# Seven small products for gate/up product 5 too, shared buffers for the small forms, and fewer sums of right operands on VectorE

## The chip, the core and the metric

The kernel runs on one core of one Trainium2 chip. A core has five engines with queues of their own: TensorE (PE; its weight loads are PEld), VectorE (DVE), ScalarE (ACT), GpSimd (POOL) and SyncE (SP). TensorE reads SBUF and writes PSUM, which here is used as eight banks of 128 x 512 float32. SyncE issues the plain loads of this kernel, GpSimd its stores and the transfers that add to what is at the destination ("accumulating"). The metric is the time of one execution in microseconds on the device, as the median of a few runs.

## The reference

```python
a = jnp.einsum("bsd,ed->bse", x, dft_hid_re)
b = jnp.einsum("bsd,ed->bse", x, dft_hid_im)
y = jnp.einsum("ts,bse->bte", dft_seq_re, a) - jnp.einsum("ts,bse->bte", dft_seq_im, b)

gate = jnp.einsum("bsd,df->bsf", x, W_gate)
up = jnp.einsum("bsd,df->bsf", x, W_up)
h = gate * (gate > 0) * up
down = jnp.einsum("bsf,fd->bsd", h, W_down)

g = sigmoid((x * gate_w).sum(-1, keepdims=True))
out = g * y + (1 - g) * down
```

x is 1 x 2048 x 512, W_gate and W_up are 512 x 1792, W_down is 1792 x 512, the sequence matrices are 2048 x 2048 and the hidden ones 512 x 512; all is float32.

## The kernel before

**Three passes for one product.** TensorE multiplies in float32r. Each operand is split into a rounded part ("h", a ScalarE cast) and the rest ("l", a VectorE subtraction of that cast), and a product of two operands is made of three matmuls (`PARTS`): l by h, h by l, h by h.

**Seven products for eight.** Every large product is made as a 2 x 2 of blocks by Winograd's form: products 1 to 7 of sums of blocks in the order `ORDER` = 1, 5, 6, 2, 7, 3, 4. Partial results are carried from one product to the next in PSUM: ScalarE "seeds" a new bank with an old one's contents (`seed`, rows c<-c), and the next product adds to it.

**Stages.** The work goes in this order: (1) `Block`: gate and up for a pair c of 128-wide blocks of the 1792 columns (c = 0 to 6) and a row half q (0 or 1), each with h = relu(gate) * up, stored to `hd` by `h_out`; (2) `SpectralBlock`: x by the hidden matrices, stored to `ad`; one more `Block`; (3) `Down`, twice: h by W_down; (4) `Joint` J1, `Sequence` S00 and S01, J3, S11, S10, J2: the sequence matrices by the results of (2). The trace names them by their tiles: c for (1), a for (2), z for `Down` and `Sequence`, jA to jH for `Joint`.

**The second level.** For c = 3 to 6 product 1 of both row halves together is itself made by seven small products: `RightOne` builds the sums of x, `One` the sums of the weights (wn, split to wnt) and runs seven products of 3 matmuls each; `WEAVE` says after which products of the block before they run. Its results `o[q]` (tile p) are copied by ScalarE into the banks of the blocks (`seed_of`, rows c<-p), which then skip product 1.

**Right operands of the last stages.** A block of `Joint` or `Sequence` needs sums of blocks of the sequence matrices. `SUMS` lists those made beforehand on the chip: 4 loads, 4 VectorE sums (p<-p,p) and 4 stores to `tb`. `DSUMS` lists those made in DRAM by GpSimd alone (`copied_sums`): 4 copies and 4 accumulating transfers from DRAM to DRAM. The key behind each is its place on the planner's scale (one unit is one matmul). A block of a `Sequence` that is in neither list is summed in place (`rights`): three loads r11, r12 and r22, three VectorE sums (r<-r,r) and one accumulating load into r11. What is in a list is loaded from tb, four loads and no sum. Next come the split casts ch and cl; ll and lh are the split of the left operands lr, loaded from ad.

**What sets the order.** All instructions are recorded as steps with a key, in matmuls. The class `Plan` gives each a due time, schedules them on the engines and on 51 buffers ("units") by its own costs, and issues them in the order of the starts it found. `AT` holds key offsets.

Of the kernel before, what the change touches and what calls it, by code (L numbers as in the profile page):

```python
# [347 lines left out]
def kernel(ctx: ExitStack, tc, xP, xG, wgu, wd, cr, ci, wri, gw, out):  # L348
# [55 lines left out]
    class Pair:  # L404


        def __init__(self, name):
            self.name, self.banks = name, None
# [19 lines left out]
    def load(o, i):  # L428
        plan.sync.dma_start(o, i)
# [88 lines left out]

    AT = {'open': (-19, 11, 33, 19, 97), 'w0': (17, 83, 110), 'x': (-192, -134, -93, -86, -59, -42, 27, 18), 'gate': (66, 44, 474), 'v': (-90, -80, -68, -38, -22, 4, 10, 42, 44), 'lw': (-246, -150, -138, -114, -112, -104), 'll': (-90, 62, 36, 96, 138, 176), 'l0': (-154, -42, -52, 32), 'l1': (-60, -118, -28, 40), 'z': (38,), 'J1': (88, 14, 76, 56, 124), 'J2': (174, 18, 40, 44, 52), 'J3': (168, 22, 62, 62, 52), 'hr': (52, 48, 61), 'rest': (26, 46), 'gated': (1880, 1930, 1968, 2012), 'xt': (-20, 26, 62), 'p': (62, 44, 32, 16), 'hs': (8, 6)}

    SUMS = {(0, 3, 1): 1764, (0, 1, 0): 865, (0, 2, 1): 665, (0, 3, 0): 965, (1, 1, 0): 1600, (1, 2, 1): 1632, (1, 5, 3): 1310, (1, 4, 2): 1070, (0, 4, 0): 489, (0, 1, 1): 125, (1, 4, 3): 1730}

    DSUMS = {(0, 2, 0): 290, (1, 2, 0): 100, (1, 3, 1): 417, (1, 3, 0): 675, (1, 1, 1): 520}

# [4 lines left out]
    def h_out(q, c, h, key):  # L529
# [16 lines left out]
        for n, t, k in ((1, h[1], 3), (3, f[0], 8), (5, f[1], 14))[:3 - q]:  # L546
            op(key + k, lambda n=n, t=t: store(hd[q, n:n + 2, :, c].rearrange("x p n -> p x n"), t.all))

    class RightOne:

        def __init__(self, key):
            self.x = buf("x011")
            self.raw = [buf(f"xt{n}") for n in range(2)]
            self.t = [[buf(f"xt{n}{y}", dtype=F32R) for y in "hl"] for n in range(2)]
            x, y, r = self.x, piece[1, "11"], self.raw
            op(key, lambda: load(x.all, xP[0, 0]))
            for n, (o, a, b) in enumerate(((r[0][:, 0], y[:, 0], y[:, 1]), (r[0][:, 1], x[:, 0], y[:, 0]),
                                           (r[1][:, 0], r[0][:, 1], y[:, 1]), (r[1][:, 1], r[1][:, 0], x[:, 1]))):
                op(key + AT["xt"][1] + 2 * n, lambda o=o, a=a, b=b: E().vector.tensor_add(o, a, b))
            for n in range(2):  # L560
                hi, lo = self.t[n]
                op(key + AT["xt"][2] + 10 * n, lambda n=n, hi=hi: E().scalar.copy(hi.all, r[n].all))
                op(key + AT["xt"][2] + 10 * n + 5, lambda n=n, hi=hi, lo=lo: E().vector.tensor_sub(lo.all, r[n].all, f32(hi.all)))

        def of(self, m):
            if m in (1, 2, 3):
                q, k = {1: (0, 0), 2: (0, 1), 3: (1, 1)}[m]
                return [X[q, 1][y][:, k] for y in range(2)]
            n, k = {7: (0, 0), 5: (0, 1), 6: (1, 0), 4: (1, 1)}[m]
            return [self.t[n][y][:, k] for y in range(2)]  # L570

    class One:

        SLOT = {5: 0, 7: 1, 6: 2, 3: 3}

        def __init__(self, w, right, key):
            self.w, self.right = w, right
            self.raw, self.t = buf("wn", [4, P]), buf("wnt", [2, 4, P], F32R)
            self.o = [buf("p") for q in range(2)]
            self.s = buf("ps")  # L580
            self.b = {}
            f, a = self.raw, lambda i, k: w.raw[0][:, i, k]
            for n, (o, x, y) in enumerate(((f[:, 0], a(1, 0), a(1, 1)), (f[:, 1], a(1, 0), a(0, 0)),
                                           (f[:, 2], a(0, 0), f[:, 0]), (f[:, 3], a(0, 1), f[:, 2]))):
                op(key - AT["p"][1] + 2 * n, lambda o=o, x=x, y=y: E().vector.tensor_sub(o, x, y))
            op(key - AT["p"][2], lambda: E().scalar.copy(self.t[:, 0], f.all))
            op(key - AT["p"][3], lambda: E().vector.tensor_sub(self.t[:, 1], f.all, f32(self.t[:, 0])))

        def left(self, m):
            if m in (1, 2, 4):  # L590
                i, k = {1: (0, 0), 2: (0, 1), 4: (1, 1)}[m]
                return [w[:, k] for w in self.w.of(1, i)]
            return [self.t[:, y, self.SLOT[m]] for y in range(2)]
# [20 lines left out]
        def evac(self, m):  # L614
            e, o, s, y, bank = E(), self.o, self.s[:, 0], self.s[:, 1], self.bank

            def seed(k, i, scale):
                self.new(k)
                e.scalar.activation(bank(k), bank(i), AF.Copy, scale=scale)

            if m == 1:
                seed("X", "A", -1.0)
            elif m == 5:
                e.scalar.copy(y, bank("B"))
            elif m == 6:
                seed("D", "X", 1.0)
                e.scalar.copy(s, bank("X"))
            elif m == 2:
                e.scalar.copy(o[0][:, 0], bank("A"))
            elif m == 7:  # L630
                seed("G", "D", -1.0)
                e.vector.tensor_add(o[1][:, 1], bank("D"), y)
            elif m == 3:
                e.vector.tensor_add(o[1][:, 0], bank("B"), s)
            elif m == 4:
                e.scalar.copy(o[0][:, 1], bank("G"))

    class Block:
# [8 lines left out]

        def run(self, order=ORDER, one=None, part=None):
            if part:
                self.part = part.o[self.q]  # L650
                for k in "AX":
                    op(plan.now, self.seed_of, k)
            for m in order:
                for i in range(2):
                    pe(6, self.product, m, i)
                    op(plan.now, self.evac, m, i)
                    if one and (m, i) in WEAVE:
                        one.run(*WEAVE[m, i])
            h_out(self.q, self.w.c, self.h, plan.now + (8 if plan.now > 270 else 100))
# [15 lines left out]

        def seed_of(self, k):
            self.ps[k].new()
            for i in range(2):
                E().scalar.copy(self.ps[k][i], self.part[:, i])

        def resume(self, key):
            op(key, self.seed_of, "X")
            self.run(ORDER[1:3] + ORDER[4:])
# [11 lines left out]
        def evac(self, m, i):  # L695
# [24 lines left out]
            elif m in (3, 7):  # L720
                o, ps, t = (h[0][:, 1], p["B"], self.s) if m == 3 else (h[1][:, 1], p["D"], self.y)
                e.vector.tensor_add(t[:, 0] if i == 0 else o, ps[i], t[:, i])
                if i:
                    e.vector.scalar_tensor_tensor(o, t[:, 0], 0.0, o, op0=OP.max, op1=OP.mult)


    WEAVE = {(7, 1): (1,), (3, 0): (6, 2), (4, 0): (5, 7), (4, 1): (3, 4)}

# [312 lines left out]
    class Sequence(Round):  # L1041
# [29 lines left out]
        def rights(self):  # L1071
# [5 lines left out]
            for jj in range(4):  # L1077
# [9 lines left out]
                for b, t in (("12", 110), ("22", 105), ("11", 90 if m else 100)):  # L1087
                    x = (6 if b == "11" else 7) if m else 5
                    op(at[x, jj] - t, lambda r=r, b=b, jj=jj: load(r[b].all, source(b, jj)))

# [278 lines left out]
    for b, f in (("11", pairs[0]), ("21", pairs[1])):  # L1369
        for k, w in zip(halves, (w0, w1)):  # L1370
# [4 lines left out]
            else:  # L1375
                op(-99, w.load, 0, f)
    for f, *a in ((x_load, 0, "12"), (w2.load, 0), (w0.load, 1), (x_load, 0, "22"), (w1.load, 1), (w2.load, 1), (lambda: load(gwt[:], gw),)):
        op(-98, f, *a)
# [35 lines left out]
    def blocks(sequence):  # L1414
        ones = {}
        for n, (c, q) in enumerate(sequence):
# [3 lines left out]
            if d > 2 and d != c:  # L1420
                if d == 3:
                    right = RightOne(plan.now + AT["xt"][0])
                base = plan.now + (60 if c < 3 else 48)
                w_prep(ws.setdefault(d, Weights(d)), base + 45, early=AT["p"][0])
                one = ones[d] = One(ws[d], right, base)
            if (c, q) == (2, 1):
# [119 lines left out]
```

## Time and profile before

| | |
|---|---|
| median of 3 runs | 775.47 us (775.25 to 776.31) |
| the profiled execution | 775.92 us; its span 774.1 us |
| granted TensorE clock | 1.000 |
| instructions on PE, DVE, ACT, POOL | 3392, 812, 713, 204 |
| HBM | read 189.01 MB, written 94.38 MB |
| TensorE busy by its pieces of the chain | c to 330, then c again to 349, z (`Down`) 349 to 482, J1 to 520, S00 and S01 to 607, J3 to 645, S11 and S10 to 732, J2 to 771 us |

All rows of the profile carry line 125, since every step is issued by one line of `Step.run`; groups are told apart by their tiles, written out<-in. The rows of the prediction come from the page, the waits (who waited, for whom, how long in all, how often), the chain that ended last, windows of the span, groups by form (count, busy time and mean ns of one, then the engine's idle time before them and what ended it), and timelines (start, length, engine, instruction).

### The profile page before, as it was taken

Reading aid. Unit: us, or ns where it says so; the run is one execution under the profiler, and the core shown is the slowest. Engines: PE = TensorE matmul, PEld = TensorE weight load, DVE = VectorE, ACT = ScalarE, POOL = GpSimd, SP = SyncE. Lnnn points to the kernel's source line nnn. Section 1 sums busy time; section 2 is a strip of 40 time slices with the busy share of each in tenths; the row PEclk is TensorE's granted clock in tenths of the full one; section 3 lists DMA queues with packets and bytes.
Section 4 is the critical chain, followed back from the end, with each engine's and each line's share of the span. In section 5 each row is a group of like instructions: output and inputs, shape, how many; then the busy total and the mean of one; then the engine's idle time right before and its main releaser. Section 6 shows DMA issues by size and latency. Waiting matters only on the chain.

```text
span 774.1 us, 10131 instructions
## 1 busy us (share of the span) xinstructions
PE 768.3 (99%) x3392; PEld 634.1 (82%) x3392; DVE 698.6 (90%) x812; ACT 500.0 (65%) x713; POOL 141.3 (18%) x204
## 2 busy tenths in 40 slices
PE   8999999999999999999999999999999999999998
PEld 6878888887888888888888888888888888888887
DVE  6999878676778976999889999999999999999997
ACT  6765474747475644686464668957567886566873
POOL 0133533343223223310202010001010001111000
PEclk9999999999999999999999999999999999999999
DMA  8765999999799999999999999999959899999994
GB/s 322 262 179 177 327 351 343 318 383 292 297 318 419 290 394 420 418 391 406 386 408 419 412 410 392 401 410 412 294 173 338 312 409 358 305 344 296 344 367 96
DMA packets 83683, 263.08 MB, mean 340 GB/s; under 512 B 8624, under 2 KB 19632, under 8 KB 83632
## 3 DMA queue, kind: packets, MB, share of 16 engines
q1 hardware_dynamic: 48048, 162.17, 54.3%
q0 software_dynamic: 35440, 100.15, 42.2%
q8 instruction: 26, 0.43, 0.2%
q14 instruction: 25, 0.20, 0.1%
q10 hardware_dynamic: 144, 0.13, 0.0%
HBM read 189.01 MB, written 94.38 MB: 366 GB/s over the span
## 4 chain that ended last, share of the span: by engine, by line
PE 90%; DVE 5%; DMA 2%; ACT 1%; issue 1%; SPq 1%; ACTq 0%; DVEq 0%
PE z L125 40%; PE c L125 26%; PE a L125 10%; PE jB L125 4%; PE jA L125 4%; DMA wr<-wgu 2%; PE jX L125 2%; PE jD L125 2%; PE jG L125 1%; DVE wr L125 1%; PE jH L125 1%; DVE h L125 1%; DVE p L125 1%; DVE xl L125 1%; SPq L125 1%
## 5 line engine op out<-in xcount | busy, mean ns | idle before, releaser
L125 PE MATMUL z<-cl,lh 128*128 128x512 f32 x452 | 175.9, 389 | 0.0
L125 PE MATMUL z<-ch,ll 128*128 128x512 f32 x452 | 175.8, 389 | 0.0
L125 PE MATMUL z<-ch,lh 128*128 128x512 f32 x452 | 175.8, 389 | 0.0
L125 DVE TENSOR_TENSOR jcl<-jr,jch 128x1024 fp32r<-128x1024 f32 x84 | 98.7, 1221 | 1.2 <-ACT jch L125 1.1
L125 PEld LDWEIGHTS z<-cl,lh 128*128 128x128 f32 x452 | 84.8, 188 | 17.8 <-DVE cl L125 0.2
L125 PEld LDWEIGHTS z<-ch,lh 128*128 128x128 f32 x452 | 84.8, 188 | 17.6
L125 PEld LDWEIGHTS z<-ch,ll 128*128 128x128 f32 x452 | 84.8, 188 | 17.6
L125 ACT CAST ch<-r 128x1024 fp32r<-128x1024 f32 x64 | 66.2, 1053 | 43.5 <-DVE r L125 30.0
L125 ACT CAST jch<-jr 128x1024 fp32r<-128x1024 f32 x84 | 84.8, 1056 | 8.7 <-PE z L125 4.0
L125 DVE TENSOR_TENSOR cl<-r,ch 128x1024 fp32r<-128x1024 f32 x64 | 77.3, 1220 | 0.8 <-ACT ch L125 0.6
L125 ACT CAST ch<-hr 128x1024 fp32r<-128x1024 f32 (+1 forms) x56 | 51.5, 942 | 29.0 <-PE z L125 17.7
L125 ACT ACTIVATE c<-c 128x512 f32<-128x512 f32 x74 | 43.0, 585 | 41.8 <-PE c L125 30.3
L125 DVE TENSOR_TENSOR cl<-hr,ch 128x1024 fp32r<-128x1024 f32 (+1 forms) x56 | 59.6, 1086 | 5.0 <-ACT ch L125 3.1
L125 DVE TENSOR_TENSOR p<-p,p 128x1024 f32<-128x1024 f32 x44 | 53.5, 1220 | 5.0 <-DMA p<-ci 2.7
L125 POOL DMA_DIRECT2D tb<-p x48 | 26.7, 555 | 142.8 <-DVE p L125 131.0
L125 PE MATMUL c<-xh,w2l 128*128 128x512 f32 x112 | 43.7, 390 | 0.2 <-ACT g L125 0.2
L125 PE MATMUL c<-xh,w1l 128*128 128x512 f32 x112 | 43.8, 391 | 0.0
L125 PE MATMUL c<-xl,w1h 128*128 128x512 f32 x112 | 43.6, 389 | 0.0
L125 PE MATMUL c<-xl,w2h 128*128 128x512 f32 x112 | 43.6, 389 | 0.0
L125 PE MATMUL c<-xh,w2h 128*128 128x512 f32 x112 | 43.6, 389 | 0.0
L125 PE MATMUL c<-xh,w1h 128*128 128x512 f32 x112 | 43.6, 389 | 0.0
L125 PE MATMUL a<-vh,xl 128*128 128x512 f32 x112 | 43.6, 389 | 0.0
(196 smaller groups left out, 1686.7 us busy)
## 6 DMA issues: line engine op xcount, KB each, us to landing
tb<-p POOLq DMA_DIRECT2D x48, 512.0 KB, 8.5
jr<-tb SPq DMA_DIRECT2D x48, 512.0 KB, 9.3
hr<-hd SPq DMA_DIRECT2D x36, 512.0 KB, 8.7
ad<-a POOLq DMA_DIRECT2D x28, 512.0 KB, 8.5
p<-cr SPq DMA_DIRECT2D x24, 512.0 KB, 8.5
tb<-ci POOLq DMA_DIRECT2D x24, 512.0 KB, 11.7
hd<-hs POOLq DMA_DIRECT2D x21, 512.0 KB, 10.6
r<-cr SPq DMA_DIRECT2D x21, 512.0 KB, 12.6
```

Of the source, the lines that this page charges most:

```text
L125: getattr(getattr(nc, self.engine), self.name)(*map(ap, self.a), **{k: ap(x) for k, x in self.k.items()})
```

## The change

Product 5 of c = 3 to 6 gets the same treatment as product 1. `RightOne` and `One` take the product's number m. The block of q = 0 weaves the seven small products of its own product 5 (`fives[c]`) between its other products, in the order 2, 6, 7, 3, 4; the block of q = 1 weaves those of the next pair's product 1 between 2, 6, 3, 7, 4. The results of product 5 come back as a second `part`, copied into bank B, so that a block of c = 3 to 6 has five products of its own.

Buffers: the sums of weights are kept in `gwt` (the gate weights are now loaded after the last block), the results share the tiles p, one of the small right operands is written over the halves of X[1, 1] and X[1, 5], which `forms_again` restores from the input (two loads, one difference, two casts, two subtractions).

Right operands: `SUMS` falls from 11 entries to 6 and `DSUMS` rises from 5 to 8; (0, 4, 0) of S00 and (1, 4, 2) of S10 are in neither list any more. `ONTO` names three blocks, (0, 0, 1) and (0, 0, 2) of S00 and (1, 0, 1) of S10, in which one of the three VectorE sums is an accumulating load into r12 instead. Many offsets of `AT` are others.

```diff
-    SUMS = {(0, 3, 1): 1764, (0, 1, 0): 865, (0, 2, 1): 665, ...
+    ONTO = {(0, 0, 1): 50, (0, 0, 2): 50, (1, 0, 1): 42}
+    SUMS = {(0, 3, 1): 1754, (0, 3, 0): 100, (1, 1, 0): 1690, (1, 5, 3): 1600, (0, 1, 1): 1582, (1, 4, 3): 1230}
...
+    def forms_again(key):
+        r = buf("x011")
+        for j in range(2):
+            op(key, lambda j=j: load(r[:, j], xP[2 + j, 0, :, 0]))
+        op(key + 30, lambda: E().vector.tensor_sub(r[:, 1], r[:, 1], r[:, 0]))
+        for j, m in enumerate((1, 5)):
+            hi, lo = (z[:, 0] for z in X[1, m][:2])
+            op(key + 30 + 8 * j, lambda j=j, hi=hi: E().scalar.copy(hi, r[:, j]))
+            op(key + 34 + 8 * j, lambda j=j, hi=hi, lo=lo: E().vector.tensor_sub(lo, r[:, j], f32(hi)))
...
     class RightOne:
-        def __init__(self, key):
+        def __init__(self, m, key, step, both=None):
...
+            if both:
+                self.t[1] = both.t[1]
+            x, y, r = self.x, X[1, m][2], self.raw
+            if m == 1:
+                op(key, lambda: load(x.all, xP[0, 0]))
+            else:
+                op(key, lambda: E().vector.tensor_add(x.all, *(f32(z.all) for z in X[0, m][:2])))
...
+            to = [(r[0].all, [z.all for z in self.t[0]]), (r[1][:, 0], [z[:, self.k] for z in self.t[1]]),
+                  (r[1][:, 1], [z[:, 0] for z in X[1, m][:2]])]
...
     class One:
-        def __init__(self, w, right, key):
+        def __init__(self, w, right, key, step):
-            self.raw, self.t = buf("wn", [4, P]), buf("wnt", [2, 4, P], F32R)
+            self.t = buf("wnt", [2, 4, P], F32R)
             self.o = [buf("p") for q in range(2)]
-            self.s = buf("ps")
...
     class Block:
-        def run(self, order=ORDER, one=None, part=None):
-            if part:
-                self.part = part.o[self.q]
+        def run(self, order=ORDER, one=None, weave=None, parts=()):
+            if parts:
+                self.part, self.y = (p.o[self.q] for p in parts)
                 for k in "AX":
-                    op(plan.now, self.seed_of, k)
+                    op(plan.now, self.seed_of, k, self.part)
             for m in order:
+                if m == 3 and parts:
+                    op(plan.now - 12 * self.q, self.seed_of, "B", self.y)
                 for i in range(2):
                     pe(6, self.product, m, i)
...
-    WEAVE = {(7, 1): (1,), (3, 0): (6, 2), (4, 0): (5, 7), (4, 1): (3, 4)}
+    WEAVE = {1: {(7, 1): (1,), (3, 0): (6, 2), (4, 0): (5, 7), (4, 1): (3, 4)},
+             5: {(2, 0): (1,), (2, 1): (6, 2), (6, 0): (5, 7), (6, 1): (3, 4)},
+             0: {(3, 1): (1,), (7, 0): (6, 2), (7, 1): (5, 7), (4, 0): (3, 4)}}
...
                 for key, o, a, b, sign in sums:
+                    if (m, self.p, jj) in ONTO and (o, a, b) == ("12", "12", "22"):
+                        key = max(key - ONTO[m, self.p, jj], at[5, jj] - 39 if not m else 0)
+                        op(key, lambda r=r, jj=jj: accumulate(r["12"].all, source("22", jj)))
+                        continue
                     op(key, lambda r=r, o=o, a=a, b=b, sign=sign: combine(r[o].all, r[a].all, r[b].all, sign))
...
-            if c in ones:
-                Block(q, ws[c]).run(ORDER[1:], one, ones[c])
-            else:
-                Block(q, ws[c]).run(ORDER, one)
+            if c not in ones:
+                Block(q, ws[c]).run(ORDER, one, WEAVE[1])
+                continue
+            if q == 0:
+                if c == 3:
+                    five = RightOne(5, plan.now + AT["xt5"][0] - 30, (10, 40 + AT["xt5"][1]), right)
+                fives[c] = One(ws[c], five, plan.now + 6, AT["p5"])
+            Block(q, ws[c]).run((2, 6, 3, 7, 4) if q else (2, 6, 7, 3, 4), one if q else fives[c], WEAVE[0 if q else 5],
+                                (ones[c], fives[c]))
...
+    forms_again(plan.now + AT["again"][0])
+    op(plan.now - 60, lambda: load(gwt.all, gw))
```

The programs differ by instructions as follows: 12 matmuls fewer; on VectorE 20 sums p<-p,p fewer, 3 sums r<-r,r more, 24 differences of 128 x 128 more and 16 others more; on ScalarE 12 seeds c<-c, 16 copies c<-p and 10 others more. SyncE issues 20 transfers fewer, GpSimd 9 more.

ScalarE at the start of the first block of c = 3, before. p_969 is the result of the small products of product 1, the c on the left are the banks of the new block.

```order
L125 COPY c_1027<-p_969 128x512
L125 COPY p_969<-c_1003 128x512
L125 COPY c_1041<-p_969 128x512
L125 COPY c_1048<-p_969 128x512
L125 CAST w3_1053<-wr3_1033 128x512
L125 COPY y_1059<-c_1030 128x512
L125 COPY y_1059<-c_1046 128x512
```

The same place in the changed program; p_981 is that result, xt0h and wnt are operands of small products, xh5 one of the overwritten halves.

```order
L125 CAST xt0h_1025<-xt0_961 128x1024
L125 CAST wnt_1033<-gwt_73 128x512
L125 COPY p_981<-c_1009 128x512
L125 COPY c_1043<-p_981 128x512
L125 COPY c_1050<-p_981 128x512
L125 ACTIVATE c_1057<-c_1046 128x512
L125 COPY c_1062<-p_981 128x512
L125 CAST xh5_563<-xt1_969 128x512
L125 ACTIVATE c_1075<-c_1057 128x512
```

The copies of product 5 to y are gone from the block; seeds of the small products (c_1057, c_1075) and casts for them stand among the block's own seeds, and the block's first product is now one that adds to a seeded bank.

VectorE at the start of S00, before, from behind the last jcl of J1. Tiles r_ come from tb, r11, r12 and r22 are summed in place.

```order
L125 TENSOR_TENSOR cl5_4685<-r_4574,ch5_4659 128x1024
L125 TENSOR_TENSOR r11_4562<-r11_4562,r12_4537 128x1024
L125 TENSOR_TENSOR r11_4588<-r11_4588,r12_4570 128x1024
L125 TENSOR_TENSOR cl5_4708<-r11_4562,ch5_4699 128x1024
L125 TENSOR_TENSOR jo1_4719<-jD_4516,js_4547 128x512
L125 TENSOR_TENSOR jo1_4719<-jB_4403,js_4547 128x512
L125 TENSOR_TENSOR cl5_4730<-r11_4588,ch5_4710 128x1024
L125 TENSOR_TENSOR r11_4604<-r11_4604,r12_4594 128x1024
L125 TENSOR_TENSOR ll7_4751<-lr7_4614,lh7_4723 128x1024
L125 TENSOR_TENSOR r12_4537<-r12_4537,r22_4550 128x1024
L125 TENSOR_TENSOR cl5_4772<-r11_4604,ch5_4755 128x1024
```

The same place in the changed program.

```order
L125 TENSOR_TENSOR r11_4579<-r11_4579,r12_4553 128x1024
L125 TENSOR_TENSOR r11_4607<-r11_4607,r12_4588 128x1024
L125 TENSOR_TENSOR cl5_4727<-r11_4579,ch5_4721 128x1024
L125 TENSOR_TENSOR cl5_4737<-r11_4607,ch5_4730 128x1024
L125 TENSOR_TENSOR r11_4633<-r11_4633,r12_4615 128x1024
L125 TENSOR_TENSOR jo1_4754<-jD_4558,js_4583 128x512
L125 TENSOR_TENSOR jo1_4754<-jB_4440,js_4583 128x512
L125 TENSOR_TENSOR cl5_4767<-r11_4633,ch5_4757 128x1024
L125 TENSOR_TENSOR r11_4652<-r11_4652,r12_4640 128x1024
L125 TENSOR_TENSOR r12_4553<-r12_4553,r22_4575 128x1024
L125 TENSOR_TENSOR cl5_4793<-r11_4652,ch5_4784 128x1024
```

All four blocks of S00 are now summed in place, so the first cl5 has two sums ahead of it and the loads of the fourth block stand ahead of the left operands (lr7, lr6) on SyncE. Up to the second cl6 of the stage VectorE has two instructions of 128 x 1024 more than before.

GpSimd at the same place, before:

```order
L125 DMA out<-z12_4453 128x1024
L125 DMA zd_70<-jo1_4719 128x1024
L125 DMA zd_70<-jo0_4628 128x1024
L125 DMA r11_4562<-cr 128x1024
L125 DMA r11_4588<-cr 128x1024
L125 DMA r11_4604<-cr 128x1024
```

And in the changed program:

```order
L125 DMA out<-z12_4482 128x1024
L125 DMA r12_4588<-cr 128x1024
L125 DMA zd_70<-jo0_4660 128x1024
L125 DMA zd_70<-jo1_4754 128x1024
L125 DMA r12_4615<-cr 128x1024
L125 DMA r11_4579<-cr 128x1024
L125 DMA r11_4607<-cr 128x1024
```

Two accumulating loads into r12 stand around the two stores of J1's results, ahead of those into r11.

More of the change, by code (lines that the diff above doesn't have):

```diff
@@ L549 @@
     class RightOne:
-        def __init__(self, key):
-            self.x = buf("x011")
+        def __init__(self, m, key, step, both=None):
+            self.m, self.x = m, buf("x011")
             self.raw = [buf(f"xt{n}") for n in range(2)]
             self.t = [[buf(f"xt{n}{y}", dtype=F32R) for y in "hl"] for n in range(2)]
-            x, y, r = self.x, piece[1, "11"], self.raw
-            op(key, lambda: load(x.all, xP[0, 0]))
+            self.k = 1 if both else 0
+            if both:
[5 more added lines that the diff above has]
+                op(key, lambda: E().vector.tensor_add(x.all, *(f32(z.all) for z in X[0, m][:2])))
@@ L557, in __init__ @@
             for n, (o, a, b) in enumerate(((r[0][:, 0], y[:, 0], y[:, 1]), (r[0][:, 1], x[:, 0], y[:, 0]),
                                            (r[1][:, 0], r[0][:, 1], y[:, 1]), (r[1][:, 1], r[1][:, 0], x[:, 1]))):
[L559 to L563, printed above, removed]
+                op(key + step[0] + 2 * n, lambda o=o, a=a, b=b: E().vector.tensor_add(o, a, b))
@@ L565, in of @@
+            to = [(r[0].all, [z.all for z in self.t[0]]), (r[1][:, 0], [z[:, self.k] for z in self.t[1]]),
+                  (r[1][:, 1], [z[:, 0] for z in X[1, m][:2]])]
+            for n, (raw, (hi, lo)) in enumerate(to):
+                op(key + step[1] + 7 * n, lambda raw=raw, hi=hi: E().scalar.copy(hi, raw))
+                op(key + step[1] + 7 * n + 5, lambda raw=raw, hi=hi, lo=lo: E().vector.tensor_sub(lo, raw, f32(hi)))
         def of(self, m):
@@ L567, in of @@
                 q, k = {1: (0, 0), 2: (0, 1), 3: (1, 1)}[m]
-                return [X[q, 1][y][:, k] for y in range(2)]
-            n, k = {7: (0, 0), 5: (0, 1), 6: (1, 0), 4: (1, 1)}[m]
-            return [self.t[n][y][:, k] for y in range(2)]
+                return [X[q, self.m][y][:, k] for y in range(2)]
+            if m == 4:
+                return [X[1, self.m][y][:, 0] for y in range(2)]
+            if m == 6:
+                return [self.t[1][y][:, self.k] for y in range(2)]
+            return [self.t[0][y][:, 0 if m == 7 else 1] for y in range(2)]
     class One:
         SLOT = {5: 0, 7: 1, 6: 2, 3: 3}
-        def __init__(self, w, right, key):
+        def __init__(self, w, right, key, step):
             self.w, self.right = w, right
-            self.raw, self.t = buf("wn", [4, P]), buf("wnt", [2, 4, P], F32R)
+            self.t = buf("wnt", [2, 4, P], F32R)
             self.o = [buf("p") for q in range(2)]
-            self.s = buf("ps")
             self.b = {}
[L582 to L587, printed above, removed]
+            raw, both = gwt.all, [self.t[:, y].rearrange("p a n -> p (a n)") for y in range(2)]
+            f, a = [gwt[:, n * P:(n + 1) * P] for n in range(4)], lambda i, k: w.raw[SLOT[right.m][0]][:, i, k]
+            for n, (o, x, y) in enumerate(((f[0], a(1, 0), a(1, 1)), (f[1], a(1, 0), a(0, 0)),
+                                           (f[2], a(0, 0), f[0]), (f[3], a(0, 1), f[2]))):
+                op(key - step[0] + 2 * n, lambda o=o, x=x, y=y: E().vector.tensor_sub(o, x, y))
+            op(key - step[1], lambda: E().scalar.copy(both[0], raw))
+            op(key - step[2], lambda: E().vector.tensor_sub(both[1], raw, f32(both[0])))
         def left(self, m):
@@ L591, in left @@
                 i, k = {1: (0, 0), 2: (0, 1), 4: (1, 1)}[m]
-                return [w[:, k] for w in self.w.of(1, i)]
+                return [w[:, k] for w in self.w.of(self.right.m, i)]
             return [self.t[:, y, self.SLOT[m]] for y in range(2)]
@@ L614, in evac @@
         def evac(self, m):
-            e, o, s, y, bank = E(), self.o, self.s[:, 0], self.s[:, 1], self.bank
+            e, o, s, y, bank = E(), self.o, self.o[1][:, 0], self.o[1][:, 1], self.bank
             def seed(k, i, scale):
@@ L656, in run @@
                     op(plan.now, self.evac, m, i)
-                    if one and (m, i) in WEAVE:
-                        one.run(*WEAVE[m, i])
+                    if one and (m, i) in weave:
+                        one.run(*weave[m, i])
             h_out(self.q, self.w.c, self.h, plan.now + (8 if plan.now > 270 else 100))
@@ L1376 @@
                 op(-99, w.load, 0, f)
-    for f, *a in ((x_load, 0, "12"), (w2.load, 0), (w0.load, 1), (x_load, 0, "22"), (w1.load, 1), (w2.load, 1), (lambda: load(gwt[:], gw),)):
+    for f, *a in ((x_load, 0, "12"), (w2.load, 0), (w0.load, 1), (x_load, 0, "22"), (w1.load, 1), (w2.load, 1)):
         op(-98, f, *a)
@@ L1414, in blocks @@
     def blocks(sequence):
-        ones = {}
+        ones, fives = {}, {}
         for n, (c, q) in enumerate(sequence):
@@ L1421, in blocks @@
                 if d == 3:
-                    right = RightOne(plan.now + AT["xt"][0])
-                base = plan.now + (60 if c < 3 else 48)
+                    right = RightOne(1, plan.now + AT["xt"][0], AT["xt"][1:])
+                base = plan.now + (60 if c < 3 else 36)
                 w_prep(ws.setdefault(d, Weights(d)), base + 45, early=AT["p"][0])
-                one = ones[d] = One(ws[d], right, base)
+                one = ones[d] = One(ws[d], right, base, AT["p"][1:])
             if (c, q) == (2, 1):
```

17 lines of the change are left out of this document (9 added, 8 removed).

## The prediction

> **What bounds the kernel now.** First the page's span, busy times and TensorE's waits.
>
> ```profile
> span 774.1 us, 10131 instructions
> PE 768.3 (99%) x3392; PEld 634.1 (82%) x3392; DVE 698.6 (90%) x812; ACT 500.0 (65%) x713; POOL 141.3 (18%) x204
> ...
> PE warm L125 <- DVE warm L125: 1.1, 1, 1.1
> PE c L125 <- ACT w0h L125: 0.8, 1, 0.8
> PE c L125 <- ACT c L125: 0.4, 1, 0.4
> PE c L125 <- ACT g L125: 0.2, 1, 0.2
> ```
>
> TensorE waits 2.5 us in the whole run, 0.6 of them (the last two rows) outside the opening, so the time is the count of matmuls times the price of one. The chain that ended last gives the price, and the places of the last stages.
>
> ```profile
> 520.28 87.04 PE z L125 x384
> 607.32 5.44 PE jA L125 x24
> ...
> 765.08 5.76 PE jH L125 x48
> ```
>
> 87.04 us / 384 = 0.2267 us. The two Sequence stages S00 and S01 fill 520 to 607. Next, the windows by stage (sum, then PE, PEld, DVE, ACT, POOL busy, clock, DMA share, GB/s).
>
> ```profile
> 107.00:254.00 147.00, 146.65 (x647) 120.85 (x646) 109.61 (x157) 88.83 (x154) 50.30 (x69) 1.00 1.05 339
> 272.00:311.00 39.00, 39.00 (x173) 32.30 (x173) 27.28 (x49) 18.68 (x35) 11.19 (x17) 1.00 1.02 414
> 272.00:556.00 284.00, 284.00 (x1254) 235.00 (x1254) 264.24 (x291) 182.85 (x249) 40.75 (x65) 1.00 1.02 401
> 349.00:482.00 133.00, 133.00 (x588) 110.00 (x587) 125.90 (x133) 83.30 (x110) 14.83 (x27) 1.00 1.02 406
> 482.00:520.00 38.00, 38.00 (x169) 31.45 (x168) 37.96 (x39) 29.09 (x38) 1.60 (x3) 1.00 1.01 401
> 520.00:607.00 87.00, 87.00 (x386) 72.03 (x385) 86.50 (x88) 59.74 (x73) 7.05 (x9) 1.00 0.89 301
> 607.00:645.00 38.00, 38.00 (x169) 31.46 (x168) 37.15 (x34) 31.47 (x38) 0.85 (x1) 1.00 1.02 394
> 610.00:752.00 142.00, 142.00 (x629) 117.56 (x628) 140.53 (x141) 101.41 (x125) 12.82 (x15) 1.00 1.04 349
> 645.00:732.00 87.00, 87.00 (x385) 72.06 (x384) 86.32 (x92) 57.94 (x74) 11.12 (x13) 1.00 1.04 326
> 732.00:768.00 36.00, 36.00 (x172) 30.31 (x172) 35.86 (x37) 22.47 (x25) 2.54 (x3) 1.00 0.84 259
> ```
>
> While c = 3 to 6 run (107 to 254), VectorE is idle for 37 us and ScalarE for 58. From 482 to 768 VectorE is idle for 2.2 us (0.04 + 0.5 + 0.85 + 0.68 + 0.14) and TensorE for nothing: the two are balanced to a microsecond. The transfers are a third full resource: a DMA share of 1.02 to 1.04 from 272 to 556 and from 610 to 752. How closely loads, ScalarE and VectorE follow each other is seen at the start of S00:
>
> ```profile
> 522.11 1.06 ACT L125 CAST lh<-lr 128x1024 fp32r<-128x1024 f32 x1 [0.58 <-DMA lr<-ad]
> 523.46 1.05 ACT L125 CAST lh<-lr 128x1024 fp32r<-128x1024 f32 x1 [0.29 <-DMA lr<-ad]
> 524.68 1.06 ACT L125 CAST lh<-lr 128x1024 fp32r<-128x1024 f32 x1 [0.17 <-DMA lr<-ad]
> ...
> 524.55 1.22 DVE L125 TENSOR_TENSOR ll<-lr,lh 128x1024 fp32r<-128x1024 f32 x1
> 525.69 1.22 DVE L125 TENSOR_TENSOR r<-r,r 128x1024 f32<-128x1024 f32 x1
> 526.82 2.36 DVE L125 TENSOR_TENSOR cl<-r,ch 128x1024 fp32r<-128x1024 f32 x2
> ...
> 537.04 1.22 DVE L125 TENSOR_TENSOR cl<-r,ch 128x1024 fp32r<-128x1024 f32 x1
> ```
>
> Casts start as loads land, 1.3 us apart. The first cl of 526.82 is ready at 528.0 (1.22 us); its matmul has 37 of the stage before it and starts at 520.28 + 37 x 0.2267 = 528.7. The cl of 537.04 is ready at 538.3, and its matmul, with 85 before it, starts at 539.6. The leads are 0.6 and 1.3 us.
>
> **The change part by part.** *Matmuls.* A product of a pair c takes 2 x 2 x 6 = 24 matmuls for both row halves, in seven small products 7 x 3 = 21. Four pairs save 12: -2.72 us. Nothing hides this, since TensorE is never idle there.
>
> *ScalarE and VectorE in the pairs.*
>
> ```profile
> L125 ACT ACTIVATE c<-c 128x512 f32<-128x512 f32 x74 | 43.0, 585 | 41.8 <-PE c L125 30.3 <-DVE y L125 6.9 <-DVE h L125 4.2
> L125 ACT COPY c<-p 128x512 f32<-128x512 f32 x38 | 21.6, 592 | 2.2 <-DVE s L125 2.0
> L125 DVE TENSOR_TENSOR wn<-wr,wn 128x128 f32<-128x128 f32 x8 | 2.3, 288 | 0.1
> L125 DVE TENSOR_TENSOR p<-p,p 128x1024 f32<-128x1024 f32 x44 | 53.5, 1220 | 5.0 <-DMA p<-ci 2.7 <-DMA p<-cr 2.1
> L125 DVE TENSOR_TENSOR r<-r,r 128x1024 f32<-128x1024 f32 x36 | 43.2, 1219 | 0.0
> ```
>
> ScalarE has 38 instructions more, nearly all 128x512: 38 x 0.59 = 22 us, under its 58 idle. VectorE gains 24 small differences and some 15 of 128x512 and loses 20 p sums (24 us): about -7 us net there. What is not hidden is latency. A half block now begins with product 2, whose second bank is seeded from the last small product by two ScalarE copies (0.59 each), with only 9 matmuls (2.04 us) between; if a 1.05 us cast stands ahead of them, that is 0.2 to 0.5 us late, at four places. Against this, the existing 0.6 us could go. Bounds -0.6 to +2 us; I take +0.3, nearest to the 0.4 of the one such wait that the trace has.
>
> *Sums of right operands.* Five quadruples of sums by VectorE go (8 transfers each), three made in DRAM come (4 copies, 4 accumulates each); two Sequence operands, (0,4,0) and (1,4,2), are no longer summed beforehand, and three accumulating loads come in their place. Net: +6 sums in the Sequence stages, -3 by accumulation, one more in S00 and two more in S10. Transfer prices, from windows with one kind, with an accumulate in DRAM, and with up to three accumulating loads among plain ones:
>
> ```profile
> 512.00:524.00 12.00, 12.00 (x55) 9.93 (x54) 11.96 (x12) 5.00 (x6) 1.06 (x2) 1.00 1.03 413
> 31.00:34.00 3.00, 3.00 (x15) 2.45 (x15) 2.96 (x5) 2.56 (x5) 0.00 (x0) 1.00 1.02 162
> 544.00:556.00 12.00, 12.00 (x55) 9.93 (x54) 12.00 (x12) 7.36 (x11) 0.00 (x0) 1.00 1.04 295
> ```
>
> Of 0.524 MB: plain 1.27 us, accumulate in DRAM 3.24. At 295 GB/s 6.75 transfers fit in 12 us; if three are accumulating, each takes (12 - 3.75 x 1.27) / 3 = 2.4 us. So transfers change by -40 x 1.27 + 12 x (1.27 + 3.24) - 2 x 1.27 + 5 x 2.4 = +13 us. The DRAM part falls before 272 (share 1.05, with idle stretches), where only p sums wait on it: 0. In S00 it does not: two more loads stand ahead of the lr rows above and one accumulating load runs beside them, 2 x 1.27 + 2.4 = 4.9 us later. Their first ll (done at 525.8) is needed after 48 matmuls of the stage, at 531.2: 5.4 us of cover. Hidden, just.
>
> *VectorE in S00.* Its order puts two instructions more (2 x 1.14, the step between the rows above) ahead of the cl whose lead was 1.3: 1.0 us late, unless VectorE enters earlier; it idled 7.1 us in 349 to 482 and can. Bounds 0 to 2.6 (1.0, and 1.6 on top if a load comes late by one plain load's 1.27 and its cast another 0.3, a lead of the rows above); I take 0.4, nearer to 0, since TensorE waits for nothing in every window from 349 on.
>
> *VectorE to the end.* From 482 it has 3 x 1.14 = 3.4 us more to do. It moves with TensorE until 311 (11.7 us idle in 272 to 311), so the -2.72 does not count against it. Cover: 2.2 us idle after 482, and its lead at the end:
>
> ```profile
> 763.07 3.49 DVE L125 TENSOR_TENSOR jcl<-jr,jch 128x1024 fp32r<-128x1024 f32 x3
> ```
>
> The last is ready at 766.6; its matmul has 22 of jH (5.76 / 48 = 0.12 us each) before it and starts at 765.08 + 2.64 = 767.7: 1.1 us. Left 0.1, bounds 0 to 3.4; with the S00 term I take 0.2.
>
> *The transfers by a page.* The Trainium skill, Perfetto Trace Analysis, Identifying the Most-Contended Engine, says that DMA occupancy misleads and HBM utilization should be read; its section Engine Utilization puts a single core's ceiling near 435 GB/s. By that, 401 GB/s (272 to 556) leaves about 8% free, an estimate, the S00 terms vanish, and the time would be 773.2. The casts that start within 0.6 us of a landing speak against it.
>
> **Sum.** -2.72 + 0.3 + 0.4 + 0.2 = -1.8 us. The profiled execution took 775.92, 0.45 above the median 775.47; so 774.1 for such an execution and 773.6 for the median.
>
> **Rivals.** *A, given back (0.30).* The S00 wait comes in full (1.0 + 0.5), 0.6 is left at the end and ScalarE's copies cost 0.5: -2.72 + 2.6, so 775.4. For: a lead of 0.6 us, and no idle time of VectorE. Against: 7.1 us idle just before.
> *B, slower (0.20).* The accumulating loads decide, in S00 and S10. They are issued by GpSimd only after VectorE's sum, and each delays the load beside it by 2.4 us. If the lr rows land over 5.4 us later than now, where I count 4.9, VectorE stands still, and having no idle time it does not recover. Price: the 2.6 of S00, and in S11 and S10 (two accumulating loads more, one plain load fewer: 2 x 2.4 - 1.27 = 3.5) what the lead of 1.1 leaves, 2.4. Time: 775.47 - 2.72 + 0.3 + 2.6 + 2.4 = 778.0; it is slower by over 0.2% as soon as the two parts together reach 4.0.
> That the matmuls aren't saved is excluded: the order has 12 fewer.
>
> **The numbers.** My forecast has 0.50. One measurement of this kernel tells about 0.2%, 1.55 us, from no change: faster is below 773.9, slower above 777.0. The forecast of 773.6 lies 0.3 inside the first; about as much of it falls above 773.9 as of A (1.5 above it) falls below. Low end: -2.72 - 0.6 gives 772.2, unlikely, so 772.4. High end: 777.4, inside B; of its 0.20 some 0.15 lies beyond, and 0.05 is below the low end. Faster 0.50, same 0.30, slower 0.20.
>
> **What would show it.** Right: 3380 matmuls, TensorE's waits outside the opening at 1 to 2 us, mostly z behind cl or ll near S00 and jcl at the end; VectorE idle under 2 us from 480 on; a higher ScalarE share before 254. Wrong: waits of c behind ScalarE over 2 us; z waiting over 3 us in S00 or S10; a load that VectorE or ScalarE waits for by microseconds there.

## The result, and the profile after

| | before | changed |
|---|---|---|
| median of 18 runs each | 775.43 us (774.68 to 776.31) | 777.15 us (776.39 to 778.41) |
| profiled execution, its span | 775.92, 774.1 us | 778.31, 776.5 us |

The ratio is 1.0023, with a 95% interval of 1.0016 to 1.0030: slower by 1.7 us, where 1.8 us of gain were forecast (773.6). The number lies in the range given (772.4 to 777.4), but on the other side of before, near a high end that was taken from rival B. The profiled execution is the second slowest of the 18; three took over 778, the others 776.39 to 777.46. A second profile, of e6 further down, shows which part of it is common.

The page of the changed kernel:

```profile
span 776.5 us, 10124 instructions
PE 768.1 (99%) x3380; PEld 632.0 (81%) x3380; DVE 697.8 (90%) x835; ACT 519.9 (67%) x751; POOL 155.0 (20%) x213
```

TensorE's waits in it (who waited, for whom, total, count, longest):

```profile
PE z L125 <- DVE cl L125: 1.0, 3, 0.4
PE jB L125 <- DVE jcl L125: 1.0, 1, 1.0
PE c L125 <- ACT g L125: 0.6, 1, 0.6
PE c L125 <- ACT w0h L125: 0.5, 1, 0.5
PE c L125 <- ACT c L125: 0.3, 1, 0.3
```

The 12 matmuls are gone, and there are two waits in the late stages that before did not have. The chain that ended last shows at which stage the gain went, here of the changed kernel:

```profile
252.05 76.16 PE a L125 x336
...
480.53 2.66 PE jA L125 x12
...
492.35 11.48 DMA jr<-tb
...
503.90 11.29 DMA r<-cr
...
515.21 18.27 DMA lr<-ad
...
533.56 20.76 DMA r<-cr
...
561.37 46.31 PE z L125 x203
607.68 5.44 PE jA L125 x24
...
645.76 87.05 PE z L125 x384
733.28 12.93 DMA jr<-cr
...
766.96 5.94 PE jH L125 x48
```

And two rows of before's:

```profile
253.64 76.16 PE a L125 x336
...
482.20 5.44 PE jA L125 x24
```

The spectral stage begins 1.6 us earlier: 2.7 saved, 1.1 lost in the pairs. J1 begins 1.7 earlier. J3 begins at 607.68, before at 607.32: S00 and S01 have lost 2.0 (written S00 below, where all of it lies). S11 and S10 lose nothing (645.76 + 87.05), and jH begins at 766.96 instead of 765.08: J2 has lost another 1.5, and 0.2 in jH. The rows of waits show only 2.0 of these 3.7 us; the starts of the stages show the whole. Five transfers stand in the chain from J1 on, loads of jr, r, lr, r and jr; before's had none after 180 us.

S00 in the changed kernel, ScalarE's casts of the left operands and VectorE (start, length, instruction, idle time before):

```profile
524.68 1.05 ACT L125 CAST lh<-lr 128x1024 fp32r<-128x1024 f32 x1 [0.19 <-DMA lr<-ad]
527.75 1.06 ACT L125 CAST lh<-lr 128x1024 fp32r<-128x1024 f32 x1 [1.06 <-DMA lr<-ad]
530.20 1.06 ACT L125 CAST lh<-lr 128x1024 fp32r<-128x1024 f32 x1
...
525.76 1.22 DVE L125 TENSOR_TENSOR ll<-lr,lh 128x1024 fp32r<-128x1024 f32 x1
...
549.83 2.43 DVE L125 TENSOR_TENSOR cl<-r,ch 128x1024 fp32r<-128x1024 f32 x2
554.41 2.36 DVE L125 TENSOR_TENSOR r<-r,r 128x1024 f32<-128x1024 f32 x2 [2.16 <-DMA r<-cr]
```

Before, the first three of these casts ran at 522.11, 523.46 and 524.68: they are now 2.6, 4.3 and 5.5 us later, and they come 2.5 to 3.1 us apart instead of 1.3. At 552 VectorE stands 2.16 us for a load of r. Windows (us, sum, PE, PEld, DVE, ACT, POOL busy, clock, DMA share, GB/s) of everything from J1 on and of S00, first the changed kernel, then before:

```profile
482.00:768.00 286.00, 284.01 (x1253) 233.66 (x1252) 282.85 (x283) 199.34 (x244) 27.56 (x34) 1.00 0.99 333
520.00:564.00 44.00, 42.98 (x186) 34.42 (x185) 41.74 (x38) 27.46 (x32) 4.92 (x7) 1.00 1.04 343
```

```profile
482.00:768.00 286.00, 286.00 (x1275) 237.32 (x1274) 283.79 (x286) 200.71 (x246) 23.16 (x29) 1.00 0.96 329
520.00:564.00 44.00, 44.00 (x196) 36.44 (x195) 43.92 (x40) 29.30 (x33) 3.64 (x5) 1.00 0.93 335
```

In S00, where the transfers had had some room, their share went from 0.93 to 1.04. VectorE is busy 2.2 us less there, as long as it stood for the load.

### The profile page after: what moved, and what is told of

The parts are those of the page before. It is cut to its first block, busy times and chain, and to the rows that moved or that the text cites. A ratio compares the mean times of both kernels' runs of the same rounds, so it can differ in the third digit from the quotient of the medians.

```text
span 776.5 us, 10124 instructions
## 1 busy us (share of the span) xinstructions
PE 768.1 (99%) x3380; PEld 632.0 (81%) x3380; DVE 697.8 (90%) x835; ACT 519.9 (67%) x751; POOL 155.0 (20%) x213
## 4 chain that ended last, share of the span: by engine, by line
PE 75%; DMA 12%; DVE 8%; ACT 2%; issue 2%; SPq 1%; DVEq 0%; ACTq 0%
PE z L125 34%; PE c L125 25%; PE a L125 10%; DMA r<-cr 4%; DMA lr<-ad 2%; DMA wr<-wgu 2%; PE jA L125 2%; DMA jr<-cr 2%; PE jB L125 2%; DVE jcl L125 2%; DMA jr<-tb 1%; DVE p L125 1%; DVE wr L125 1%; PE jH L125 1%; PE jG L125 1%
## 5 line engine op out<-in xcount | busy, mean ns | idle before, releaser
L125 ACT ACTIVATE c<-c 128x512 f32<-128x512 f32 x86 | 50.1, 586 | 36.9 <-PE c L125 27.9
L125 DVE TENSOR_TENSOR r<-r,r 128x1024 f32<-128x1024 f32 x39 | 46.9, 1219 | 2.2 <-DMA r<-cr 2.2
L125 PE MATMUL a<-vl,xh 128*128 128x512 f32 x112 | 43.6, 389 | 0.0
L125 PE MATMUL a<-vh,xh 128*128 128x512 f32 x112 | 43.6, 389 | 0.0
L125 ACT COPY a<-a 128x512 f32<-128x512 f32 x40 | 23.0, 581 | 27.7 <-PE a L125 21.6
L125 POOL DMA_DIRECT2D hd<-h x28 | 23.2, 859 | 88.7 <-DVE h L125 75.4
```

The source lines that it names most:

```text
L125: getattr(getattr(nc, self.engine), self.name)(*map(ap, self.a), **{k: ap(x) for k, x in self.k.items()})
```

## Experiments

Each kernel is ordered anew by the planner, so a run also carries small moves. Differences are taken to the median of before in the same set of runs; the changed kernel stands at +1.7.

### Which half of the change

The change without its new lists, and the lists without the small products:

```diff
 e1 (on the changed kernel): SUMS, DSUMS of before; ONTO = {}
 e2 (on the kernel before):  SUMS, DSUMS, ONTO of the change, with its branch in `rights`
```

> The changed kernel with the lists of before (SUMS, DSUMS, no ONTO): product 5 by small products alone. Transfers theory (the time went to the later arrival of the loads of S00 and of S11/S10, which the lists caused): 12 matmuls less (-2.7) and about 1.1 of new waits in the pairs c, so 773.8 to 774.3, with S00 back at 87.0 us. VectorE theory (three more sums in the late stages): the same, since those three sums are gone as well. A third theory, that the pairs themselves eat the gain (20 sums of p are back on VectorE there): 775.4 or more, with waits of c of 3 us.

> The kernel before with the new lists alone (SUMS, DSUMS, ONTO), no small products of product 5. Transfers theory and VectorE theory: the 2.0 lost in S00 and about 1.7 lost up to the end come without the 2.7 gained, 778 to 779.5. If instead S00 lost because TensorE came there 1.7 us earlier than the transfers, which run full from 272 on, could follow: about 1.7 less is lost, 777 or less.

e1 took 811.61 us (ratio 1.0467, 1.0452 to 1.0481), e2 779.70 (1.0056, 1.0044 to 1.0069). So the lists alone cost 4.3 us, and the small products and the new offsets on top of them bring 2.6. The 4.3 is an upper figure, since e2 keeps the offsets of before. In e2's trace S00 takes 88.7 us and S11 with S10 88.5, each 87.0 before, though TensorE enters J1 only 0.4 us earlier than before; so the late stages lose even where TensorE is hardly early. In e1 the first two expectations missed, and the third had the place right, the pairs, but by far not the size. Its largest wait, of TensorE:

```profile
PE c L125 <- ACT p L125: 15.0, 2, 8.4
```

The lists can't be taken back, it seems. Two of their blocks tell whether that holds for these alone:

```diff
 e7: ONTO = {}, SUMS  + (0, 4, 0): 489, (1, 4, 2): 1070
 e8: ONTO = {}, DSUMS + (0, 4, 0): 290, (1, 4, 2): 890
```

> The changed kernel with (0, 4, 0) and (1, 4, 2) back in SUMS at their old places and ONTO empty: the Sequence stages have the sums, loads and accumulating loads of before, and the pairs c carry 16 transfers and 8 sums of p more. Theory of two binding resources: S00 back at 87.0 us and the end as before, 773.8 to 774.6 if the pairs hold it. If the pairs have no room for the loads, stores and buffers: new waits of c, 776 or more.

> As the run before, with the two blocks made in DRAM by GpSimd (DSUMS) instead: no buffer and no sum of VectorE, but about 2 x 18 us of transfers more before 272, where the share is 1.05 already. Same late stages: 773.8 to 774.6 if these transfers find gaps; if the transfers before 272 are a bound, loads of the pairs come late (waits of c) or the blocks are ready late and S00 loses instead, 776 or more.

799.65 (1.0312, 1.0294 to 1.0330) and 797.41 (1.0284, 1.0269 to 1.0298). In e7 ScalarE's copies of the small results stand for a store, behind which their buffer comes free: GpSimd issued it at 120.2 us, after four transfers of the lists that landed up to 132.0:

```profile
133.33 1.07 ACT L125 COPY p<-c 128x512 f32<-128x512 f32 x2 [12.02 <-DMA hd<-hs]
```

In e8 the pairs lose less and the stages behind them more: spectral waits of 3.8 and 2.0 us, 5.1 of z behind cl. The waits are not all of these losses: the granted clock was 0.90 from 100 to 200 us in e1 and 0.83 from 100 to 150 in e7, against 1.00 in the changed kernel. S00 and S10 lose nothing in e7 and e8, as expected, but TensorE also enters J1 more than 20 us later there. At these places, then, the pairs with the small products of product 5 have room neither for the buffers nor for the transfers of two blocks more; other places weren't tried.

### Transfers or VectorE

```diff
 e3 (additions left out):
-                        op(key, lambda r=r, jj=jj: accumulate(r["12"].all, source("22", jj)))
                         continue
 e4 (additions left out), ahead of the sum's op(...):
+                    if (m, self.p, jj, o + a + b) in ((0,0,0,"111122"), (1,0,2,"121222"), (1,0,2,"111112")):
+                        continue
```

> The changed kernel without the three accumulating loads of ONTO (their addition is left out: those three blocks are used without r22 in r12). VectorE has as many sums as in the changed kernel, about 7 us of transfers less (3 x 2.4). Transfers theory: the 2.0 of S00 goes and part of the 1.7 at the end, 774 to 775.5. VectorE theory: unchanged, 776.7 to 777.5.

> The changed kernel without three sums of VectorE, one of block (0, 0, 0) in S00 and two of (1, 0, 2) in S10 (their additions are left out); all transfers stay. Transfers theory: S00 still loses most of its 2.0, since VectorE stood 2.2 us for a load there, and the gain is at most the end's, 776 to 777. VectorE theory: the 3.4 us of work taken away come back, up to the 3.7 lost, 773.5 to 774.5.

778.74 (1.0041, 1.0028 to 1.0055) and 778.65 (1.0040, 1.0028 to 1.0053): both slower than the changed kernel, which no theory had. Their traces show TensorE ending 1.4 and 0.6 us earlier than the changed kernel's, and 1.9 and 1.7 more behind it: ScalarE's very last instruction, the issue of the last store, took 1.97 and 1.77 instead of 0.37 us. Both have three instructions (semaphore waits) more on ScalarE. Three more instructions were tried by themselves, and in e5, e10, e11, e12 and e14 the effect was kept out by eight such copies; in the other runs the last issue took 0.37 us without them:

```diff
 e6: ahead of plan.run
+    pads = [small.tile([P, 1], F32, name=f"pad{n}") for n in range(2)]
+    nc.vector.memset(pads[0], 0.0)
+    for n in range(3): nc.scalar.copy(pads[1], pads[0])
 e11 = e3 and e12 = e4, with range(8)
```

> The changed kernel, with three copies of one element per partition at the head of ScalarE's program and nothing else. Block theory (in the runs without three accumulating loads and without three sums ScalarE's last transfer took 1.97 and 1.77 us instead of 0.37 because three instructions more on ScalarE put it into a new 8 KB block of its program, fetched only then): 778.6 to 779.0, the last issue near 1.8 us and a fetch of 8192 bytes at it. Rival (that tail belongs to the work left out): 777.0 to 777.3 and 0.37 us.

e6 took 779.18 (1.0050, 1.0036 to 1.0065), 1.8 above the changed kernel and a little more than expected. ScalarE's end in the changed kernel, then in e6:

```profile
772.98 0.37 ACT L125 COPY jo<-jH 128x256 f32<-128x256 f32 x1 [2.49 <-PE jH L125]
773.38 0.37 ACTq L125 DMA_DIRECT2D out<-jo  x1
```

```profile
772.30 0.37 ACT L125 COPY jo<-jH 128x256 f32<-128x256 f32 x1 [2.50 <-PE jH L125]
772.71 2.25 ACTq L125 DMA_DIRECT2D out<-jo  x1
```

The trace's transfers show a read of 8192 bytes on the instruction queue at 773.3 us in e6, inside that issue; in the changed kernel it comes at 774.9, behind it, and in e11 with eight copies at 760.0, long before an issue that took 0.37. The block theory holds. Up to there e6 is the changed kernel a second time, and its waits are

```profile
PE jB L125 <- DVE jcl L125: 1.0, 1, 1.0
PE c L125 <- ACT g L125: 0.7, 1, 0.7
...
PE z L125 <- DVE cl L125: 0.4, 1, 0.4
```

so the 2.16 us for a load of r and two of three waits of z were this one execution's, while jB's wait came again.

> The run without the three accumulating loads once more, with eight small copies ahead on ScalarE. Block theory: its 778.74 falls by about 1.9 to 776.6 to 777.0, the last issue back at 0.37 us; so that without the transfers alone little is won (about 0.4), since VectorE sets the end.

> The run without the three sums once more, with eight small copies ahead on ScalarE. Block theory: 778.65 falls by about 1.7 to 776.7 to 777.2; without the sums alone little is won, since the loads set the end.

776.99 (1.0021, 1.0011 to 1.0031) and 777.17 (1.0023, 1.0013 to 1.0032), 1.6 and 1.8 above before. By the medians three accumulating loads less, or three sums less, are each worth nothing. Then both together:

```diff
 e5: e3 and e4 in one, with range(8)
```

> The changed kernel without the three accumulating loads of ONTO and without the three sums of VectorE of (0, 0, 0) and (1, 0, 2) (all these additions left out); eight copies of one element per partition are put at the head of ScalarE's program, so that its last instructions do not fall at the start of a new 8 KB block of its program (see the run with three copies). Theory of two binding resources (VectorE and the transfers each set about the same time in S00 and at the end, so that removing one alone brought nothing): the 2.0 of S00 and most of the 1.7 at the end come back at once, 773.5 to 774.5. If something else holds the end (the order of VectorE's last instructions): 775.5 or more.

774.55 us (0.9987, 0.9978 to 0.9996): 1.1 below before, 2.8 better than the changed kernel. Its waits are

```profile
PE warm L125 <- DVE warm L125: 1.1, 1, 1.1
PE c L125 <- ACT w0h L125: 0.8, 1, 0.8
PE c L125 <- ACT g L125: 0.3, 1, 0.3
PE c L125 <- ACT c L125: 0.3, 1, 0.3
PE c L125 <- DVE w L125: 0.2, 1, 0.2
```

with none of z or jB. The windows from 482 to 768 tell why one alone did not do, e11, e12 and e5 in this order:

```profile
482.00:768.00 286.00, 284.87 (x1264) 235.14 (x1262) 284.37 (x284) 199.29 (x244) 24.83 (x31) 1.00 0.96 327
```

```profile
482.00:768.00 286.00, 284.81 (x1267) 235.50 (x1266) 281.27 (x282) 197.64 (x244) 27.53 (x34) 1.00 0.98 333
```

```profile
482.00:768.00 286.00, 286.00 (x1281) 237.48 (x1280) 282.55 (x283) 198.44 (x245) 24.83 (x31) 1.00 0.96 328
```

Without the accumulating loads VectorE is busy for 284.4 of 286 us and sets the end. Without the sums it is idle for 4.7 us, and TensorE still stands 1.2. VectorE's and ScalarE's waits there, of e12:

```profile
DVE cl L125 <- ACT ch L125: 4.1, 3, 2.7
...
ACT ch L125 <- DMA r<-tb: 5.2, 2, 3.6
```

VectorE stands for casts, and the casts for loads. Without both, TensorE waits for nothing in these stages. Last, both in one place at a time:

```diff
 e13: only (0,0,1), (0,0,2) of the loads and (0,0,0) of the sums left out
 e14: only (1,0,1) of the loads and the two sums of (1,0,2) left out, with range(8)
```

> The changed kernel without the two accumulating loads of (0, 0, 1) and (0, 0, 2) and without one sum of (0, 0, 0): both resources relieved in S00 alone (these additions left out). If S00 and the end each cost on their own: S00's 0.7 comes back and the end keeps its 1.7, 776.3 to 776.7. If S00's lateness is what arrives at the end: 774.5 to 775.2.

> The changed kernel without the accumulating load of (1, 0, 1) and without two sums of (1, 0, 2): both resources relieved in S10 alone; eight small copies ahead on ScalarE. If the two places cost on their own: the end's 1.7 comes back, S00's 0.7 stays, 775.2 to 775.7. If S00's lateness arrives at the end: 776.5 to 777.2.

776.16 (1.0009, 1.0000 to 1.0018) and 775.33 (1.0001, 0.9992 to 1.0010): 1.0 and 1.8 better than the changed kernel, together the 2.8 of e5. By the medians the two places cost on their own, though e13's interval just meets the changed kernel's; that the end's loss is S00's, handed on (774.5 to 775.2 for e13), is excluded. The traces show the places, in us from the first matmul of a stage to the first of the next (J2 up to the first of jH):

| | before | changed | e6 | e11, no loads | e12, no sums | e5, neither | e13, S00 | e14, S10 |
|---|---|---|---|---|---|---|---|---|
| S00 and S01 | 87.0 | 89.1 | 87.7 | 87.6 | 87.0 | 87.1 | 88.4 | 87.7 |
| J2 | 32.6 | 34.2 | 34.1 | 34.2 | 34.4 | 32.6 | 33.9 | 32.6 |

At the end neither loads nor sums alone help, and both in S10 bring everything back. In S00 the sum alone does it, and 0.7 is what e6 and e14 lose, which have S00 as in the changed kernel. One trace each is thin: e12's is its fastest execution (775.96) and e13's its slowest (777.59). In e13's TensorE waits 1.1 us for another cl of S00, so the 1.0 that its median wins is not seen in its trace, and how it comes about stays open.

### The same sums on GpSimd

```diff
 e9: ONTO = {}; e10: ONTO as in the change
+                    if (m, self.p, jj, o + a + b) in POOL:   # e9: six sums, those of e3 and e4; e10: those of e4
+                        op(key, lambda ...: (E().gpsimd.tensor_add if sign > 0 else E().gpsimd.tensor_sub)(r[o].all, r[a].all, r[b].all))
+                        continue
...
+        elif engine == "gpsimd" and name in ("tensor_add", "tensor_sub"):   # the planner's cost
+            self.work = 0.2 + n * 0.00205078
```

e10 has the eight copies as well. The planner counts 2.3 us for such a sum (n is 1024).

> The changed kernel with ONTO empty and six sums of right operands on GpSimd instead of VectorE: the three that ONTO made by accumulating loads, and those of (0, 0, 0) and (1, 0, 2). VectorE's and the transfers' work of the run without both (774.55), with the whole computation. Theory of two binding resources: 774.5 to 775.3, below before, as long as a sum of 128 x 1024 on GpSimd takes under some 4 us. If GpSimd's sums take longer, or hold up VectorE, or its queue holds up the accumulating loads behind them: 776 or more.

> The changed kernel with its accumulating loads as they are and only the three sums of (0, 0, 0) and (1, 0, 2) on GpSimd; eight small copies ahead on ScalarE. Theory of two binding resources: as the run without three sums but with the tail as usual, 776.5 to 777.2, about as the changed kernel. VectorE alone: 774.5.

788.85 (1.0179, 1.0165 to 1.0193) and 781.69 (1.0083, 1.0069 to 1.0097). GpSimd and VectorE at one place of e9, then VectorE's sums in all (count, busy, mean ns), of e9 and of the changed kernel:

```profile
517.63 3.30 POOL L128 TENSOR_TENSOR r<-r,r 128x1024 f32<-128x1024 f32 x1 [11.63 <-DVE cl L128]
...
518.60 3.42 DVE L128 TENSOR_TENSOR r<-r,r 128x1024 f32<-128x1024 f32 x1
```

```profile
L128 DVE TENSOR_TENSOR r<-r,r 128x1024 f32<-128x1024 f32 x36 | 53.5, 1495 | 0.0
```

```profile
L125 DVE TENSOR_TENSOR r<-r,r 128x1024 f32<-128x1024 f32 x39 | 46.9, 1219 | 2.2 <-DMA r<-cr 2.2
```

A sum takes 3.3 us there, and a VectorE sum that runs beside it takes 3.42, where the changed kernel's take 1.22 on average: VectorE stands while GpSimd works. The sum is not taken off VectorE but made dearer. The Trainium skill, SBUF — State Buffer, Who interferes with whom, says that a VectorE instruction with two SBUF inputs and a GpSimd one that reads SBUF exclude each other; this trace agrees. No complete kernel tried here beats before.

## Why the prediction was wrong, point by point

**Matmuls, -2.72.** Right: 3380 run, and at the same price (87.05 us for 384 in S11 and S10).

**ScalarE in the pairs, +0.3 (bounds -0.6 to 2).** Mis-sized: 1.1. TensorE doesn't wait for the seeds from p; its largest wait there is one of 0.6 us for another copy. ScalarE's queue (changed kernel) and the matmul that waits:

```profile
113.08 1.05 ACT L125 CAST w1h<-wr 128x1024 fp32r<-128x1024 f32 x1 [0.42 <-DVE wr L125]
114.04 0.59 ACT L125 ACTIVATE g<-c 128x512 f32<-128x512 f32 x1
...
114.68 0.50 PE L125 MATMUL c<-xt0h,wnt 128*128 128x512 f32 x1 [0.60 <-ACT g L125]
```

A cast that waits for VectorE stands ahead of the copy that frees the bank. That this cast makes the copy late is argued, not shown: another order there was not tried. The sum counted ScalarE's idle time as cover, but not what it queues behind.

**S00, +0.4 (bounds 0 to 2.6).** Right in place and mis-sized: 0.7 in e6 and e14, 2.0 in the profiled execution, which also had a late load of r. e6's wait is at the matmul that the prediction named, the one with 85 of the stage before it, and it is for VectorE's cl:

```profile
537.65 1.22 DVE L125 TENSOR_TENSOR cl<-r,ch 128x1024 fp32r<-128x1024 f32 x1
...
538.92 0.50 PE L125 MATMUL z<-cl,lh 128*128 128x512 f32 x1 [0.38 <-DVE cl L125]
```

e6's chain holds no transfer at all behind 480 us, and without one of its sums VectorE is in time (e12). The left operands were late, by 2.6, 4.3 and 5.5 us where 4.9 was estimated, since not one but two accumulating loads run among the lr loads (issued at 516.9 and 522.0, landed at 526.1 and 534.9). But the first ll was ready at 527.0, 1.2 later than before, and TensorE waits for no ll: that cover held.

**The end, +0.2 (bounds 0 to 3.4).** This is the step that failed. It set 3.4 us of sums against "2.2 us idle after 482" and a lead of 1.1. The idle time was no cover: in before 1.7 of the 2.2 us are VectorE standing for casts, and in e12, where casts stand for loads, it has 4.7 and the end gains nothing. And S10's 3.5 us of transfers were priced in rival B alone, though they were as sure as the sums. By e14 the end costs 1.8: VectorE comes to J2 late, and TensorE waits there for jcl. Sums and loads make it together, since J2 is back at 32.6 us only without both (e14, e5).

**The sum.** With -2.72, 1.1, 1.0 (e13) and 1.8 (e14) it gives +1.2 against +1.7 measured. The other 0.5 is not placed: before's trace is of an execution 0.5 above its median, and in e6's the pairs lost 1.8 instead of 1.1.

**The rivals.** B named the mechanism of the end, accumulating loads beside a VectorE that can't recover, and took it for that of S00 as well, where the late left operands held up no matmul. Its 778.0 was 0.9 too high, and 0.20 too little for it.

**The rule on HBM utilization.** The Trainium skill, Perfetto Trace Analysis, Identifying the Most-Contended Engine, has HBM utilization read instead of DMA occupancy. The prediction's 773.2 was worked out from that. Here the measurement decides against it: S00 moved 343 GB/s, far under the 435 that the page's section Engine Utilization gives, and the six lr loads issued from 510 to 518 us took 17.3 us from issue to landing (median), where before they took 12.9; it was the DMA share of 1.04 that told it.

## What to carry to other kernels

Where two resources are full together, taking work from either alone can show no gain; relieve both at once, at one place at a time, to see what the place costs. The idle time of a nearly full engine is no cover for more work on it where it is the engine's standing for transfers. A cost that is as sure as the others belongs in the sum, not in a rival alone. And one trace can be of an odd execution: a second one of nearly the same kernel told which waits are common.

## What the runs showed of the hardware

Three more instructions at the head of ScalarE's program cost 1.8 us: its last instruction took 2.25 us instead of 0.37, and a read of 8192 bytes on the instruction queue falls inside it (e6; the last issues of e3 and e4 took 1.97 and 1.77). With eight more the read comes earlier and the cost is gone (e11), so the read block is taken for the next one of ScalarE's program. GpSimd's sum of 128 x 1024 takes 3.05 us on average (e9), and VectorE's sums stand for it, 3.42 us instead of 1.22.
